# Weight loads of five down products issued by GpSimd instead of SyncE

## The chip, the cores and the metric

The kernel runs on one core of a Trainium2 chip. Its time is the device time of one execution in microseconds, as the median of several runs. A profiled execution gives, beside its time, the span from its first to its last instruction and a trace of all engines: TensorE (PE in the profile), VectorE (DVE), ScalarE (ACT), GpSimd (POOL) and SyncE (SP), and of the 16 DMA engines that move data between HBM and the core's memory for all of them.

## The reference, cut to what matters

```python
def _B_ref(x, W_gate, W_up, W_down):          # D = 1024, F = 3584
    gate = jnp.einsum("bsd,df->bsf", x, W_gate)
    up = jnp.einsum("bsd,df->bsf", x, W_up)
    gate = gate * (lambda x, dt: x.astype(dt))(gate > 0, gate.dtype)
    h = gate * up
    return jnp.einsum("bsf,fd->bsd", h, W_down)
...
x = A_x                                        # 1 x 2048 x 1024, bfloat16
x = x + _A_ref(_layernorm(x, axis=-1), A_wqkv, A_wo)
x = x + _B_ref(_layernorm(x, axis=-1), B_W_gate, B_W_up, B_W_down)
x = x + _A_ref(_layernorm(x, axis=-1), A_wqkv, A_wo)
x = x + _B_ref(_layernorm(x, axis=-1), B_W_gate, B_W_up, B_W_down)
return x
```

Layer A is a linear attention with 32 heads, layer B a gated MLP. The kernel counts its four layers from 0, so the last layer, a B, is layer 3.

## The kernel before, in words

The residual x (2048 rows) stays in the core's memory, with rows sent away to HBM and brought back where the room is needed. A B layer goes over the rows in two chunks c of 1024. For each chunk, `glu` runs over 14 blocks u of 256 columns of F, two hidden parts per block, and computes h transposed; then `down` multiplies h by W_down. All large products are cut by Strassen's scheme (seven products of quarters in place of eight): a weight block is therefore loaded as its raw quarters and as sums of quarters, and the sums that were made in an earlier layer are read back from HBM (`tgu` for the gate and up weights, called tg and tu in the trace; `td` and `dd` for W_down).

A chunk's down phase consists of seven outer products, which for layer 3 stand in the order "11", "T2", "T1", "T3", "22", "21", "T4" (`order_d`). A plain one reads its weights in two loads of 896 KB (`product`, line 1434). A deep one is cut by the scheme once more (`deep`, line 1468): it reads its weights in four loads, three of 896 KB and one of 448 KB (`load_deep`, line 1047), and each load serves two of its seven groups of matmuls, the last one serves one. For layer 3, chunk 0, the products T1, 22, T4 and 21 are deep and 11, T2 and T3 are plain.

The weights of all layers come through one ring (`_Ring`, line 24): a list of loads in the order of use, of which at most five may be in the core at a time. Before a product uses entry i of the list, `free_before` issues the loads up to i + 4; each new load takes a slot that an earlier entry has given up, and the instruction that issues it waits on its engine until TensorE has read that entry. When "21" uses its last entry, T4's last load is issued; when T4 uses its entries, the gate and up weights of the next chunk's first block are issued (`load_gu`, line 1197: the raw part at line 1198, the sums at line 1202).

All these loads are issued by SP, in the order in which the program writes them. In the same queue of SP stand, in this stretch, the transposes of the normalized rows for the second chunk (`ln_turn`, line 423), which wait for ScalarE, and a few reads for inner products (line 1138). The transposed rows are summed on the DVE (`sums_x`, line 1272) for the next chunk's first gate product, `vg`. GpSimd multiplies one quarter of h in each block of `glu` (line 1381) and, in the last layer's down phases, issues most of the output stores (`onto`, line 1464), each of which waits for a DVE addition (line 1463). Work that is not bound to a place in the matmuls is put into a list of delayed jobs (`_Later`) that `later.tick()` runs. The tile framework allots the slots and the semaphores and sets each engine's order of instructions.

Of the kernel before, what the change touches and what calls it, by code (L numbers as in the profile page):

```python
# [12 lines left out]
F16 = mybir.dt.float16  # L13
# [79 lines left out]
class _Net:  # L93
# [889 lines left out]
    def plan_B(self, l):  # L983
        for c in range(2):
            for u in range(self.U):
                for w in "gu":
                    self.ring.add((l, c, w, u), lambda t, w=w, u=u, first=(l == 1 and c == 0),
                                  d=self.is_inner(l, c, u): self.load_gu(t, w, u, first, d))
            for p in self.order_d(l, c):
                if self.is_deep(l, c, p):  # L990
                    for e in range(4):
                        self.ring.add((l, c, p, e), lambda t, p=p, e=e: self.load_deep(t, p, e))
                    continue
                for h in range(2):
                    src = self.src_d(p, slice(h * self.U // 2, (h + 1) * self.U // 2))
                    self.ring.add((l, c, p, h), lambda t, src=src: self.nc.sync.dma_start(
                        out=t[:, 0:self.U // 2, :].bitcast(src.dtype), in_=src))

    T_AT = {"T1": 0, "T3": 1, "T4": 2, "T2": 3}
# [44 lines left out]
        return t[:, :, :].rearrange("p a b -> p (a b)")[:, 0:n].rearrange(  # L1044
            "p (m k n) -> p m k n", m=2, n=NW // 2)

    def load_deep(self, t, p, e):
        n = min(2, 7 - 2 * e)
        self.nc.sync.dma_start(out=self.deep_view(t)[:, 0:n, :, :].bitcast(F16),
                               in_=self.dd[p][:, 2 * e:2 * e + n, :, :])  # L1050

    def load_dd(self, p):
# [755 lines left out]
```

## Time and profile before

| what | value |
|---|---|
| median of 3 runs | 1442.72 us |
| lowest and highest of them | 1442.53, 1443.81 us |
| the profiled execution's own time | 1441.07 us |
| its span | 1439.3 us |
| granted clock | 1.000 |
| DMA traffic over the span | 339.14 MB, 236 GB/s on average |

The span is 1.77 us shorter than the profiled execution's time, and that time is 1.65 us below the median of the runs. In the rows that follow, a timeline's first number is the start in microseconds from the span's start, the second the duration, and a bracket at the end tells how long the engine had been idle and what ended that. "SPq" marks an instruction that SP's queue issues. A row "A <- B: x, n, y" says that A waited for B for x us in all, n times, y at the longest. A DMA's time "to landing" runs from its issue to the moment when all its bytes have arrived.

### The profile page before, as it was taken

Reading aid. Unit: us, or ns where it says so; the run is one execution under the profiler, and the core shown is the slowest. Engines: PE = TensorE matmul, PEld = TensorE weight load, DVE = VectorE, ACT = ScalarE, POOL = GpSimd, SP = SyncE. Lnnn points to the kernel's source line nnn. Section 1 sums busy time; section 2 is a strip of 40 time slices with the busy share of each in tenths; the row PEclk is TensorE's granted clock in tenths of the full one; section 3 lists DMA queues with packets and bytes.
Section 4 is the critical chain, followed back from the end, with each engine's and each line's share of the span. In section 5 each row is a group of like instructions: output and inputs, shape, how many; then the busy total and the mean of one; then the engine's idle time right before and its main releaser. Section 6 shows DMA issues by size and latency. Waiting matters only on the chain.

```text
span 1439.3 us, 21517 instructions
## 1 busy us (share of the span) xinstructions
PE 1426.7 (99%) x7763; PEld 744.3 (52%) x7790; DVE 1052.8 (73%) x2035; ACT 626.0 (43%) x1145; POOL 309.6 (22%) x220
## 2 busy tenths in 40 slices
PE   9999999999999999999999999999999998999998
PEld 4444444444455444545654444445554584555557
DVE  7978698788685666559778885765766874766895
ACT  7872564333334234332058626633442443444301
POOL 1453860010100010110031577410111021111102
PEclk9999999999999999999999999999999999999999
DMA  9950787998559999866983118988878699985575
GB/s 287 239 162 8 174 208 204 291 320 289 195 195 310 353 348 331 273 219 214 293 274 95 60 28 255 284 271 256 263 238 298 204 299 335 314 230 173 191 261 183
DMA packets 366620, 339.14 MB, mean 236 GB/s; under 512 B 110065, under 2 KB 326001, under 8 KB 365489
## 3 DMA queue, kind: packets, MB, share of 16 engines
q1 hardware_dynamic: 357936, 314.95, 73.1%
q10 hardware_dynamic: 7136, 18.88, 3.5%
q0 software_dynamic: 1440, 3.93, 0.8%
q8 instruction: 61, 1.00, 0.3%
q14 instruction: 47, 0.38, 0.1%
HBM read 248.25 MB, written 64.82 MB: 218 GB/s over the span
## 4 chain that ended last, share of the span: by engine, by line
PE 93%; DVE 4%; ACT 1%; issue 1%; DMA 1%; SPq 0%; DVEq 0%; ACTq 0%
PE ps L506 11%; PE yu L1301 9%; PE yg L1301 9%; PE dy L1443 8%; PE xu L1301 6%; PE xg L1301 6%; PE i L1154 5%; PE dx L1443 4%; PE ps L789 4%; PE zu L1301 3%; PE zg L1301 3%; PE my L588 3%; PE dy L1485 2%; PE mv L588 2%; PE mx L588 2%; PE dyT L1485 2%
## 5 line engine op out<-in xcount | busy, mean ns | idle before, releaser
L1301 PEld LDWEIGHTS <-w 128*128 128x128 f16 (+1 forms) x2768 | 270.3, 98 | 299.6 <-issue 4.0
L506 PE MATMUL ps<-w,xnT 128*128 128x512 bf16 x768 | 169.8, 379 | 0.2 <-DVE pq L452 0.2
L1381 POOL TENSOR_TENSOR h<-m5u,m5g 128x512 f16<-128x512 f32 x28 | 37.1, 1326 | 426.8 <-DVE m5u L1377 265.5
L506 PEld LDWEIGHTS <-xnT 128*128 128x128 bf16 x768 | 74.4, 98 | 89.8 <-issue 1.8
L1301 PE MATMUL xg<-xnT,w 128*128 128x512 f16 x448 | 115.4, 379 | 0.2 <-DVE yg L1341 0.2
L1301 PE MATMUL xu<-xnT,w 128*128 128x512 f16 x448 | 115.0, 379 | 0.0
L1485 PEld LDWEIGHTS <-h 128*128 128x128 f16 x1064 | 104.1, 98 | 13.3 <-issue 0.2
L1381 POOL TENSOR_TENSOR h<-c22u,c22g 128x512 f16<-128x512 f32 x28 | 35.6, 1271 | 290.2 <-DVE c22u L1377 237.5
L1301 PE MATMUL yu<-s,w 128*128 128x512 f16 x376 | 96.5, 379 | 0.5 <-DVE zu L1357 0.5
L1301 PE MATMUL yg<-s,w 128*128 128x512 f16 x376 | 96.6, 379 | 0.0
L449 ACT ACTIVATE e<-e,eps 128x512 f32<-128x512 f32 x128 | 91.0, 720 | 3.2
L736 POOL TENSOR_TENSOR kvc<-pq,kvc 128x1024 f32<-128x1024 bf16 x32 | 78.5, 2454 | 53.1 <-DVE den L741 32.8
L1443 PEld LDWEIGHTS <-h 128*128 128x128 f16 x560 | 54.8, 98 | 64.9
L789 PE MATMUL ps<-T,pqT 128*128 128x512 bf16 x374 | 83.0, 379 | 0.5
L1328 DVE TENSOR_TENSOR h<-yu,r 128x512 f16<-128x512 f32 x56 | 38.7, 691 | 54.5 <-PE yu L1301 54.5
L1325 ACT ACTIVATE r<-yg 128x512 f32<-128x512 f32 x56 | 33.4, 597 | 100.3 <-PE yg L1301 100.3
L527 POOL TENSOR_TENSOR kvc<-kvc,slab 128x512 f32<-128x512 f32 x46 | 57.2, 1249 | 76.0 <-DVE slab L452 72.7
L448 ACT ACTIVATE e<-ps 128x512 f32<-128x512 f32 x92 | 54.3, 590 | 29.1 <-PE ps L506 28.5
L1154 PEld LDWEIGHTS <-x 128*128 128x128 f16 x504 | 49.3, 98 | 33.5 <-issue 1.9
L1325 ACT ACTIVATE r<-zg 128x512 f32<-128x512 f32 x56 | 32.9, 587 | 76.0 <-PE zg L1301 76.0
L748 POOL TENSOR_TENSOR pq<-pq,den 128x1024 bf16<-128x1024 bf16 x32 | 61.2, 1911 | 6.8 <-DVE den L743 6.8
L1443 PE MATMUL dy<-w,h 128*128 128x512 f16 x280 | 61.6, 379 | 0.0
(286 smaller groups left out, 2660.7 us busy)
## 6 DMA issues: line engine op xcount, KB each, us to landing
w<-in_B_W_gate_dram SPq DMA_DIRECT2D x56, 512.0 KB, 6.1
w<-in_B_W_up_dram SPq DMA_DIRECT2D x56, 512.0 KB, 5.8
w<-ddT SPq DMA_DIRECT2D x21, 896.0 KB, 6.5
w<-dd SPq DMA_DIRECT2D x21, 896.0 KB, 5.9
w<-td SPq DMA_DIRECT2D x18, 896.0 KB, 5.5
x<-away SPq DMA_DIRECT2D x30, 512.0 KB, 7.7
away<-x SPq DMA_DIRECT2D x24, 512.0 KB, 6.7
dd<-dd SPq DMA_DIRECT2D x21, 448.0 KB, 5.6
```

Of the source, the lines that this page charges most:

```text
L449: self.last_exp = nc.scalar.activation(out=e, in_=e, func=ACT.Exp, scale=-1.0, bias=self.eps6[:, 0:1])
L506: nc.tensor.matmul(by_row(ps), lhsT=self.xnT[l, l_q][:, kt, j * P:(j + 1) * P], rhs=w[:, kt, :].rearrange("p (b i d) -> p i b d", i=R, d=H ...
L588: nc.tensor.matmul(banks[j], lhsT=A(i)[:, j * P:(j + 1) * P], rhs=B(i), start=start and i == 0, stop=i == NS - 1, skip_group_check=True)
L736: nc.gpsimd.tensor_tensor(out=prod, in0=pq_of[sc, j], in1=zrow, op=ALU.mult)
L748: nc.gpsimd.tensor_tensor(out=heads(pq), in0=heads(pq), in1=den[:, :].unsqueeze(2).to_broadcast([P, D // HD, HD]), op=ALU.mult)
L789: nc.tensor.matmul(ps, lhsT=pqT[sc][:, g, j * P:(j + 1) * P], rhs=T[g // 4][:, g % 4, n2 * NW:(n2 + 1) * NW], start=(g == 0), stop=(g == G ...
L1154: nc.tensor.matmul(b[:, w, :], lhsT=B[p][:, w, k, :], rhs=A[p][:, k, :], start=start and w == 0 and k == 0, stop=k == 1, skip_group_check= ...
L1301: nc.tensor.matmul(ps, lhsT=W[w][m][:, k, :], rhs=A[m][:, k, :], start=start and k == 0, stop=k == 3, skip_group_check=True)
L1325: self.last_relu = nc.scalar.activation(out=out, in_=ps, func=ACT.Relu)
L1381: nc.gpsimd.tensor_tensor(out=h[:, 3, :], in0=V["u"], in1=V["g"], op=ALU.mult)
L1443: nc.tensor.matmul(banks[j], lhsT=A(k)[:, j * P:(j + 1) * P], rhs=w[:, i, :], start=start and k == 0, stop=k == self.U - 1, skip_group_che ...
L1485: nc.tensor.matmul(out, lhsT=A[i // 2][:, i % 2, j * P:(j + 1) * P], rhs=B[m][:, i, :], start=start and i == 0 and j == 0, stop=i == NK - ...
```

## The change

In the last layer's first chunk the loads of five of the seven down products, T1, T3, 22, 21 and T4, are issued by GpSimd's queue instead of SP's: four loads for each of the deep ones and two for T3, 18 in all. The loads of 11 and T2, all loads of other layers and chunks, the gate and up weights and the transposes stay on SP. Bytes, slots, order of use and arithmetic are as before.

```diff
+            queue = lambda p: self.nc.gpsimd if (l, c) == (3, 0) and p not in ("11", "T2") else self.nc.sync
             for p in self.order_d(l, c):
                 if self.is_deep(l, c, p):
                     for e in range(4):
-                        self.ring.add((l, c, p, e), lambda t, p=p, e=e: self.load_deep(t, p, e))
+                        self.ring.add((l, c, p, e), lambda t, p=p, e=e, q=queue(p): self.load_deep(t, p, e, q))
                     continue
                 for h in range(2):
                     src = self.src_d(p, slice(h * self.U // 2, (h + 1) * self.U // 2))
-                    self.ring.add((l, c, p, h), lambda t, src=src: self.nc.sync.dma_start(
+                    self.ring.add((l, c, p, h), lambda t, src=src, q=queue(p): q.dma_start(
                         out=t[:, 0:self.U // 2, :].bitcast(src.dtype), in_=src))
...
-    def load_deep(self, t, p, e):
+    def load_deep(self, t, p, e, queue):
         n = min(2, 7 - 2 * e)
-        self.nc.sync.dma_start(out=self.deep_view(t)[:, 0:n, :, :].bitcast(F16),
+        queue.dma_start(out=self.deep_view(t)[:, 0:n, :, :].bitcast(F16),
                                in_=self.dd[p][:, 2 * e:2 * e + n, :, :])
```

## The prediction

> **What bounds the kernel now.** I read the cores and the busy shares first, then who TensorE waited for over the whole span, and then the stretch of the change in the timelines of PE, SP and POOL.
>
> ```profile
> core 0: 1439.3 us, clock 1.000
> ```
>
> ```profile
> PE 1426.7 (99%) x7763; PEld 744.3 (52%) x7790; DVE 1052.8 (73%) x2035; ACT 626.0 (43%) x1145; POOL 309.6 (22%) x220
> ```
>
> TensorE is busy for 1426.7 of 1439.3 us at the full clock, so only its few waits can be won. They are listed by length; the first two carry this case:
>
> ```profile
> PE vg L1301 <- DMA w<-tg: 2.1, 1, 2.1
> PE vu L1301 <- DMA w<-tu: 1.6, 1, 1.6
> ```
>
> Each happens once. The timeline of PE shows where (the third product of "21" starts at 1171.94, the first of "T4" at 1176.52, the one that needs T4's third load at 1182.63, the one that needs its fourth at 1185.69):
>
> ```profile
> 1171.94 1.69 PE L1485 MATMUL dy<-w,h 128*128 128x256 f16 x14
> ...
> 1176.52 1.69 PE L1485 MATMUL dxT<-w,h 128*128 128x256 f16 x14
> ...
> 1182.63 1.69 PE L1485 MATMUL dyT<-w,h 128*128 128x256 f16 x14
> 1184.16 1.69 PE L1485 MATMUL dzT<-w,h 128*128 128x256 f16 x14
> 1185.69 1.69 PE L1485 MATMUL dyT<-w,h 128*128 128x256 f16 x14
> 1189.47 1.04 PE L1301 MATMUL vg<-s,w 128*128 128x512 f16 x4 [2.09 <-DMA w<-tg]
> 1190.35 1.03 PE L1301 MATMUL xg<-xnT,w 128*128 128x512 f16 x4
> 1192.93 1.04 PE L1301 MATMUL vu<-s,w 128*128 128x512 f16 x4 [1.56 <-DMA w<-tu]
> ```
>
> The down phase ends at 1185.69 + 1.69 = 1187.38. Then the last layer's second chunk opens with two waits on its first gate and up sums: 2.09 + 1.56 = 3.65 us. That is all this change can win, 0.25% of the time. In SP's queue over the same stretch:
>
> ```profile
> 1165.71 0.45 SPq L1049 DMA_DIRECT2D w<-ddT  x1
> 1166.25 0.39 SPq L1138 DMA_DIRECT2D x<-tg  x1
> 1168.87 0.32 SPq L1049 DMA_DIRECT2D w<-ddT  x1
> 1169.43 4.32 SPq L423 DMA_TRANSPOSE xnT<-xnb  x1
> 1173.84 1.67 SPq L1049 DMA_DIRECT2D w<-ddT  x2
> 1175.60 3.95 SPq L423 DMA_TRANSPOSE xnT<-xnb  x1
> 1179.64 1.43 SPq L1198 DMA_DIRECT2D w<-in_B_W_gate_dram  x1
> 1181.12 3.85 SPq L1202 DMA_DIRECT2D w<-tg  x1
> 1185.07 0.41 SPq L1198 DMA_DIRECT2D w<-in_B_W_up_dram  x1
> 1185.53 0.61 SPq L1202 DMA_DIRECT2D w<-tu  x1
> ```
>
> The four T4 loads (w<-ddT), the last transposes and the gated weights share one queue in order. The gate's loads leave at 1179.64 and 1181.12, though the slot they take is the one that "21" gives up when T4 starts, at 1176.52; tu leaves only at 1185.53. SP is held mostly inside long issues (3.95, 3.85), so by the queue's backlog rather than by the count of its instructions. The same stretch in windows (last two numbers: DMA share and GB/s):
>
> ```profile
> 1156.00:1168.00 12.00, 12.00 (x111) 10.67 (x110) 11.73 (x33) 8.15 (x17) 3.40 (x5) 1.00 1.07 307
> 1168.00:1180.00 12.00, 11.96 (x110) 10.58 (x109) 6.93 (x15) 5.82 (x11) 2.85 (x4) 1.00 1.07 323
> 1180.00:1193.00 13.00, 9.35 (x77) 7.13 (x76) 6.92 (x14) 1.50 (x3) 2.85 (x4) 1.00 1.12 323
> ```
>
> The 16 DMA engines are full (share over 1, since packets overlap) up to the moment when tu lands. The line of busy tenths for 1180 to 1192, 0.3 us a digit, has one hole, about three digits long, just as the last transpose drains:
>
> ```profile
> DMA  9969959999999000599999999999889999899898
> ```
>
> So the bytes ahead of tu, not only their order, set when it lands.
>
> **The change part by part.** Five products move: T1, 22, 21 and T4 with four loads each and T3 with two, 18 issues, from SP to POOL. Bytes, slots, and the instructions of PE, DVE and ACT stay. Products "11" and "T2" stay on SP.
>
> *Off SP.* 18 issues of 0.3 to 0.7 us go. What matters is the end: without the two w<-ddT rows at 1173.84 the last transpose can leave about 1.7 us earlier, the gate's load at the slot's release, about 1176.6 instead of 1179.64, and up and tu once T4's first load has been used by two groups, at 1176.52 + 2 x 1.53 = 1179.6, so about 1180.4 instead of 1185.53. If tu then took as long to land as now (1192.93 - 1185.53 = 7.4) it would be there at 1187.8, in time, and the 3.65 us would be gone. That is the gain's end. The other end is nothing: the DMA engines are full, so everything due before vu still has to pass first and tu lands at 1192.9 as now. I am nearest to the second, by the windows: a reordering inside a full resource doesn't shorten the sum. The DVE sums that vg also needs are no obstacle:
>
> ```profile
> 1186.11 0.43 DVE L1272 TENSOR_TENSOR s<-xnT 128x512 f16<-128x512 f16 x1 [1.05 <-DMA xnT<-xnb]
> ```
>
> They end at 1186.54, before 1187.38, and come earlier if the transposes do.
>
> *Onto POOL.* POOL does no arithmetic in this phase; it issues 16 output stores, each of which waits for the DVE. As issue costs I take a store's:
>
> ```profile
> L1464 POOL DMA_DIRECT2D out_dram<-xo x16: 540/710/725, 1151.5 to 1189.0; - x16
> ...
> DMA to landing us min/median/max: 3.8/5.8/7.8
> ```
>
> 18 x 0.71 = 12.8 us of POOL, beside everything, if POOL has nothing else to do; if it had, its stores would go out that much later, and nobody waits for their landing but the program's end, 250 us on. What the move does cost is position: a load now stands behind the stores written before it. Two cases are short:
>
> ```profile
> 1162.74 0.71 POOL L1464 DMA_DIRECT2D out_dram<-xo  x1 [6.13 <-DVE xo L1463]
> ...
> 1173.57 0.71 POOL L1464 DMA_DIRECT2D out_dram<-xo  x1 [5.90 <-DVE xo L1463]
> ```
>
> The third load of "21" stands behind the store at 1162.74, so it leaves at 1163.45 and is wanted at 1171.94: 8.5 us. T4's third load leaves behind the store at 1173.57, at 1174.3, and is wanted at 1182.63: 8.3 us. The loads between stand behind stores too, or only behind a slot, and have as much or more. T1, T3 and the first of "22" are issued in a stretch without stores and lie beside the long products T2 and T3.
>
> How long does such a load take from POOL? No row shows 896 KB on that queue. Over the 16 deep loads on SP, and over T4's four alone:
>
> ```profile
> DMA to landing us min/median/max: 3.3/7.0/10.0
> ```
>
> ```profile
> L1049 SPq DMA_DIRECT2D w<-ddT x4: 319/386/710, 1165.7 to 1175.2; - x4
> ...
> DMA to landing us min/median/max: 8.6/9.3/10.0
> ```
>
> T4's third load, issued at 1173.84, lands 8.6 later at 1182.4, 0.2 before it is wanted: even now there is no slack left. Bounds for POOL: below, 3.3, the quickest on SP; above, the slowest store, 7.8, plus the 768 KB more than its 128 KB at 307 GB/s, 2.6, together 10.4. I take 9.3, the same size under the same load. Each pass of the ring of five (once for "21", once for T4) is then late by at most 9.3 - 8.4 = 0.9 us, 1.8 in all. TensorE reaches the gate's first product at 1189.2 instead of 1187.38 and finds tg there or nearly so (before: 1189.47); tu comes at 1192.9 as the full DMA engines allow. The two small waits in T4 stand in for the first one at vg. At 10.4 the lateness is 2 x 2.0 = 4.0 against the 3.65 that it replaces: +0.4. At 3.3 nothing is late.
>
> *Weighed against the skill.* The rows: with the DVE busy for 11.73 of 12 us (1156 to 1168) POOL's five issues took 3.40 us, 0.68 each; with it busy for 6.92 of 13 (1180 to 1193) four took 2.85, 0.71 each. The DVE does not hold them up. From the rows alone nothing is added. The Trainium skill, SBUF — State Buffer, in its box on the DVE-blocks-DMA trap, says that a DMA issued from GpSimd cannot have its descriptors written while the DVE runs a two-port fast-mode instruction; its example grows from about 0.62 to about 3.1 us. By that figure (an estimate from that page) each load would come some 2.5 us later and the sum would be about +3 us; the rows above don't show it for small stores.
>
> **The sum**, against the profiled execution: span 1439.3, and 1441.07 with what lies around it; the median of the three runs, 1442.72, is 1.65 above that execution. Off SP: 0 (to -3.65). Onto POOL: up to 1.8 us of new waits inside T4 and "21", in place of the old ones at the gate. Net 0: 1441.07 as a profiled time, 1442.7 as a median.
>
> **The rivals.**
>
> *The whole stall goes.* The queues serve each other's gaps, T4's loads stay in time and tu is there at 1187.8: 1442.72 - 3.65 = 1439.1. For it: SP's issues of 3.95 and 3.85 us, the hole in the DMA line, POOL stores that land in a median of 5.8 beside SP loads that take 9.3. Against it: DMA share at 1.07 to 1.12. The Trainium skill, DMA: Bandwidth & Descriptors, under queues, rings and completion order, has each DMA engine take turns between the queues by packet; by that rule T4's loads would pass the transposes in SP's queue, which would help this rival.
>
> *The load is slow from POOL, slower than before.* One mechanism: issue to landing of an 896 KB load on POOL's queue, in the stretch from 1156 to 1186. Lateness is twice what exceeds 8.4 us, less the 3.65 that it replaces; it reaches +2.9 us at 8.4 + (3.65 + 2.9) / 2 = 11.7 us. At 12.5 it gives 2 x 4.1 - 3.65 = +4.6, 1447.3. For it: no slack in T4 now, in-order stores ahead. Against: the bound of 10.4.
>
> *Slow issue on POOL.* The rows price an issue of 128 KB only. If the issue grew with the bytes, 896 KB would take 7 x 0.71 = 5.0 us, 4.3 more, and the load would land after 9.3 + 4.3 = 13.6: 2 x 5.2 - 3.65 = +6.8, 1449.5. Against it: 0.68 and 0.71 us at a full and at a half busy DVE, and SP's issues of the same loads at 0.3 to 0.7 us. The Trainium skill's trap, weighed above, would work in this place. It counts with the slower cases.
>
> **How the numbers follow.** 0.2%, about 2.9 us, is what a measurement of this kernel can tell from no change. No change within it: 0.58. The whole stall or nearly all of it gone: 0.17. Slow from POOL: 0.20, and the slow issue 0.05, so 0.25 for slower. The time is that of the likeliest, 1442.7, whose own range is 1440 to 1445. The range over the cases reaches down to 1439.1, where the stall is used up, and up to 1447, which leaves out the worst of the slow landing and the slow issue.
>
> **What would show it.** Right: 18 w loads as POOL issues of about 0.7 us; up and tu leaving SP near 1180; the waits on tg and tu smaller; new waits of TensorE on T4's or 21's loads (w<-ddT, w<-dd) of under 2 us together; the second chunk's first vu at about 1192.9. Wrong: POOL's loads landing in over 11.7 us or in under 8; an issue on POOL of several us; vu before 1190; POOL's loads ahead of the stores that I put before them; a wait elsewhere in the span that was not there.

## The result, and the profile after

The changed kernel is slower. Its median is 1450.27 us (11 runs, 1447.1 to 1455.89) against 1442.53 us for the kernel before (11 runs, 1440.29 to 1443.81): a ratio of 1.006, 95% interval 1.0046 to 1.0073; the medians lie 7.7 us apart. The ratios, here and below, go by all runs and not by the medians, and leave out one run that was far slower than the others of its kernel (3480.02 us, in experiment 2). The profiled execution took 1449.57 us. The lines of kernel.py behind the edit are one higher than before (L1464 is the DVE's addition, L1465 the store, L1486 a deep product's matmul, L1302 the gate's and up's). The cores view of the kernel after:

```profile
core 0: 1447.7 us, clock 0.998
```

The span grew by 1447.7 - 1439.3 = 8.4 us. Who TensorE waited for over the whole span, after the change:

```profile
PE vg L1302 <- DMA w<-tg: 2.7, 1, 2.7
PE dyT L1486 <- DVE xo L1464: 2.3, 1, 2.3
PE dyT L1486 <- DMA w<-ddT: 1.6, 1, 1.6
...
PE vu L1302 <- DMA w<-tu: 1.3, 2, 1.2
```

The two waits at the gate are still there (2.7 and 1.2, before 2.1 and 1.6), and two new ones stand ahead of them, inside T4. The timeline of PE of the kernel after, from T4's third load to the gate, and the last matmul of the span:

```profile
1184.60 1.70 PE L1486 MATMUL dyT<-w,h 128*128 128x256 f16 x14 [1.56 <-DMA w<-ddT]
...
1190.08 1.69 PE L1486 MATMUL dyT<-w,h 128*128 128x256 f16 x14 [2.25 <-DVE xo L1464]
1194.47 1.04 PE L1302 MATMUL vg<-s,w 128*128 128x512 f16 x4 [2.70 <-DMA w<-tg]
1195.34 1.86 PE L1302 MATMUL xg<-xnT,w 128*128 128x512 f16 x4
1198.37 1.89 PE L1302 MATMUL vu<-s,w 128*128 128x512 f16 x4 [1.17 <-DMA w<-tu]
1200.05 1.91 PE L1302 MATMUL xu<-xnT,w 128*128 128x512 f16 x4
1201.76 1.26 PE L1302 MATMUL xg<-xnT,w 128*128 128x512 f16 x4
1202.86 1.03 PE L1302 MATMUL yg<-s,w 128*128 128x512 f16 x4
...
1441.79 0.93 PE L1486 MATMUL dvT<-w,h 128*128 128x256 f16 x7
```

The rows of the kernel before that answer to the last two:

```profile
1195.53 1.03 PE L1301 MATMUL yg<-s,w 128*128 128x512 f16 x4
...
1434.48 0.93 PE L1485 MATMUL dvT<-w,h 128*128 128x256 f16 x7
```

So yg starts 7.33 us later (1202.86 - 1195.53), and so does the last matmul (1441.79 - 1434.48 = 7.31): nothing between them costs anything. The 8.4 us divide like this:

- Waits. 1.56 + 2.25 + 2.70 + 1.17 = 7.68 us in place of 2.09 + 1.56 = 3.65: **+4.0**.
- Clock. Four matmuls of 128x512 take 1.03 us at the full clock; here groups of four take 1.86, 1.89 and 1.91, and the granted clock from 1193 to 1199 is 0.70 (before: 1.00). From vg to vu it was 3.46 us before with a wait of 1.56, so 1.90 of work; now 3.90 with a wait of 1.17, so 2.73: 0.83 more. From vu to yg it was 2.60, now 4.49: 1.89 more. Together **+2.7**.
- The end. From the last matmul's end to the end of the span it was 1439.3 - 1435.41 = 3.9 us, now 1447.7 - 1442.72 = 5.0: **+1.1**.
- The rest, 8.4 - 4.0 - 2.7 - 1.1 = 0.6 us. Of it 0.24 lies ahead of T4's third load (the group ahead of that load's starts at 1181.35, in the kernel before at 1181.11). The other part lies in T4's two waits: each row overlaps the next by 0.16 us while nothing waits, so that the starts move by 1.73 and 2.42 us where the rows give 1.56 and 2.25 as idle.

Where do the waits come from? The issues are as meant. The timeline of POOL of the kernel after has T4's third and fourth load at 1172.44 and 1175.70, each of 0.55 us and not held up by a store:

```profile
1172.44 0.55 POOL L1050 DMA_DIRECT2D w<-ddT  x1 [2.48 <-PE dx L1486]
1173.80 0.72 POOL L1465 DMA_DIRECT2D out_dram<-xo  x1 [0.81 <-DVE xo L1464]
...
1175.70 0.55 POOL L1050 DMA_DIRECT2D w<-ddT  x1
```

TensorE, which waits for the third, goes on at 1184.60: 12.1 us from issue to landing. The transposes in SP's queue are slower still. The timeline of SP of the kernel after (the first row holds the last two of the eight transposes), and below it the landing times of the last six transposes, as the line's own view gives them:

```profile
1169.67 9.63 SPq L423 DMA_TRANSPOSE xnT<-xnb  x2
1179.39 0.53 SPq L1135 DMA_DIRECT2D x<-gi  x1
1180.09 1.96 SPq L1199 DMA_DIRECT2D w<-in_B_W_gate_dram  x1
1182.10 5.63 SPq L1203 DMA_DIRECT2D w<-tg  x1
...
1188.40 2.18 SPq L1203 DMA_DIRECT2D w<-tu  x1
```

```profile
DMA to landing us min/median/max: 5.7/7.8/16.8
```

SP issues tu at 1188.40, not near 1180 as the change meant, and 2.9 us later than before, since it is held in the issue of the last transpose and in tg's. tg leaves at 1182.10, 1.0 us later than before (1181.12), and takes 12.3 us to land (before: 8.3). The DVE is held too. Its additions `xo` take their room from the same buffers as the rows that the transposes read, and wait until a transpose has let one go. Two rows of the DVE's timeline, the second of which ends TensorE's wait of 2.25:

```profile
1186.59 0.69 DVE L1464 TENSOR_TENSOR xo<-x,dxT 128x512 bf16<-128x512 f32 x1 [4.34 <-DMA xnT<-xnb]
1189.34 0.69 DVE L1464 TENSOR_TENSOR xo<-x,dyT 128x512 bf16<-128x512 f32 x1 [2.06 <-DMA xnT<-xnb]
```

So weights and transposes came late together, though no bytes were added. The windows of the kernel after (last three numbers: granted clock, DMA share, GB/s) show the DMA engines as full as before, moving less:

```profile
1168.00:1180.00 12.00, 11.96 (x110) 10.58 (x109) 7.17 (x15) 5.84 (x11) 4.60 (x8) 1.00 1.15 263
1180.00:1193.00 13.00, 7.96 (x70) 6.49 (x68) 5.70 (x12) 0.60 (x1) 2.27 (x4) 1.00 1.09 284
1193.00:1199.00 6.00, 3.36 (x10) 1.09 (x11) 1.12 (x4) 1.18 (x2) 0.57 (x1) 0.70 1.11 360
```

263 and 284 GB/s stand in place of 323 and 323. In slices of 0.6 us from 1168 to 1192 the row of GB/s shows how that comes about, first of the kernel after, then of the kernel before:

```profile
GB/s 356 367 312 440 419 375 413 391 423 491 399 324 219 61 39 47 37 50 29 65 75 126 61 373 360 369 317 361 425 344 195 265 138 87 362 335 363 328 290 324
```

```profile
GB/s 336 295 40 11 136 358 351 473 423 372 554 308 382 466 481 197 293 340 223 428 504 360 369 410 388 312 19 7 200 318 292 335 382 423 319 337 341 304 405 382
```

After the change ten slices in a row, from 1175.8 to 1181.8, lie at 29 to 126 GB/s; I call this the crawl. Before, there are two dips of two slices each. The DMA queues of the kernel after from 1175.4 to 1181.4 (packets, MB, share of 16 engines) tell what the engines were busy with; a packet counts, with its whole duration, where it starts:

```profile
q1 hardware_dynamic: 702, 0.17, 116.0%
q0 software_dynamic: 44, 0.25, 22.9%
```

q1 is SP's queue, q0 POOL's. In these 6 us the transposes' packets of 256 bytes take all the engines' time: 1.16 x 16 x 6.0 us / 702 = 159 ns for each on average. POOL's queue, with the rest of T4's weights in it, moves 0.25 MB in 44 packets, one for every 16 of the transposes'. From 1150 to 1168, beside POOL's loads of "21" and T4's first, the queue of SP, which then held little but transposes, looks like this in the same kernel:

```profile
q1 hardware_dynamic: 5654, 1.40, 48.8%
```

That is 0.488 x 16 x 18.0 / 5654 = 25 ns a packet. Slow packets aren't new, though. SP's queue in the second dip of the kernel before, from 1183.6 to 1184.8:

```profile
q1 hardware_dynamic: 48, 0.02, 143.0%
```

1.43 x 16 x 1.2 / 48 = 572 ns each, but for 48 packets only. So a dip of some 1.2 us belongs to the kernel before as well; new is a stretch of 6 us.

### The profile page after: what moved, and what is told of

The parts are those of the page before. It is cut to its first block, busy times and chain, and to the rows that moved or that the text cites. A ratio compares the mean times of both kernels' runs of the same rounds, so it can differ in the third digit from the quotient of the medians.

```text
span 1447.7 us, 21559 instructions
## 1 busy us (share of the span) xinstructions
PE 1430.5 (99%) x7790; PEld 743.9 (51%) x7790; DVE 1052.1 (73%) x2035; ACT 626.3 (43%) x1145; POOL 319.4 (22%) x238
## 4 chain that ended last, share of the span: by engine, by line
PE 89%; DVE 5%; DMA 2%; issue 2%; ACT 1%; POOL 1%; SPq 0%; DVEq 0%; POOLq 0%; ACTq 0%
PE ps L506 11%; PE yu L1302 9%; PE yg L1302 9%; PE dy L1444 7%; PE xu L1302 6%; PE xg L1302 6%; PE i L1155 5%; PE dx L1444 4%; PE ps L789 4%; PE zg L1302 3%; PE zu L1302 3%; PE my L588 3%; PE mv L588 2%; PE mx L588 2%; PE dyT L1486 2%; PE vu L1302 2%
## 5 line engine op out<-in xcount | busy, mean ns | idle before, releaser
L1302 PEld LDWEIGHTS <-w 128*128 128x128 f16 (+1 forms) x2768 | 270.8, 98 | 302.3 <-issue 6.8
L1302 PE MATMUL xg<-xnT,w 128*128 128x512 f16 x448 | 116.5, 382 | 0.2 <-DVE yg L1342 0.2
L1302 PE MATMUL xu<-xnT,w 128*128 128x512 f16 x448 | 115.9, 381 | 0.0
L1486 PEld LDWEIGHTS <-h 128*128 128x128 f16 x1064 | 104.0, 98 | 17.6 <-issue 2.4
L1302 PE MATMUL yu<-s,w 128*128 128x512 f16 x376 | 96.5, 379 | 0.5 <-DVE zu L1358 0.5
L1302 PE MATMUL yg<-s,w 128*128 128x512 f16 x376 | 96.6, 379 | 0.0
```

The costliest lines, as they stand in the source:

```text
L1302: nc.tensor.matmul(ps, lhsT=W[w][m][:, k, :], rhs=A[m][:, k, :], start=start and k == 0, stop=k == 3, skip_group_check=True)
L1486: nc.tensor.matmul(out, lhsT=A[i // 2][:, i % 2, j * P:(j + 1) * P], rhs=B[m][:, i, :], start=start and i == 0 and j == 0, stop=i == NK - ...
```

## The experiments

The first theory: the transposes in SP's queue and T4's loads in another queue, in flight together, make the crawl (crossing theory). Rivals: the new order of SP's queue, in which a read of 512 KB (x<-gi) now stands ahead of the gate's weights; and GpSimd's queue as such, slow for loads of this size. The kernel before, run beside them, had medians of 1441.82 us (the first four), 1441.67 (the next four) and 1441.87 (the last four).

**1. The change without transposes.** The eight transposes of the second chunk are plain copies of the same bytes in the same pieces of 256 bytes; they leave the transposition out.

```diff
+        if (layer, q // 2) == (3, 1):
+            nc.sync.dma_start(out=self.xnT[layer, q][:, :, j * P:(j + 1) * P],
+                              in_=xn[:, :].rearrange("p (k r) -> p k r", r=P))
+            return
         nc.sync.dma_start_transpose(out=self.xnT[layer, q][:, :, j * P:(j + 1) * P], in_=xn)
```

> The changed kernel, but the eight transposes of the last layer's second chunk are plain copies of the same rows on the same queue (256 KB each, runs of 256 bytes), so that chunk computes with rows that are not turned. Crossing theory (transposes in SP's queue and weight loads in POOL's queue together bring the DMA engines to a crawl): the crawl at 1176 to 1182 is gone, no load of POOL takes over 10 us, TensorE's waits at the end of the down phase are 4 us or less and the time is 1441 to 1445. GpSimd theory (loads from POOL are slow in themselves): T4's loads still take 12 us and the time stays at 1448 to 1452. Order theory (the read of x<-gi that moved ahead of the gate's weights is the loss): that order stays, so 1448 to 1452 too.

1441.54 us, ratio 0.9996 (0.9987 to 1.0006). All 18 loads still leave from POOL, and the crawl is gone. Its windows:

```profile
1168.00:1180.00 12.00, 11.96 (x111) 10.56 (x109) 8.02 (x18) 6.25 (x11) 5.52 (x9) 1.00 1.05 375
1180.00:1193.00 13.00, 10.77 (x89) 8.31 (x87) 6.94 (x15) 1.78 (x3) 2.86 (x4) 1.00 1.06 365
```

GpSimd's queue as such is not slow: without transposes T4's loads land in 6.7 to 8.0 us, and TensorE waits for none of the 18.

**2. The kernel before without transposes.** The same edit in the kernel before.

> The kernel before with the same eight plain copies in place of transposes (the second chunk of the last layer computes with rows that are not turned): the measure for the run above. All theories: 1438 to 1443, that is, no more than the 3.65 us of the two waits can be won. If plain copies are as dear as transposes, no change.

1438.57 us, ratio 0.9979 (0.9969 to 0.9988). So the change beside plain copies still costs 1441.54 - 1438.57 = 3.0 us, 0.2%. The two profiles, 3.6 us apart in their spans, show 1.1 us of it at the end and waits at the gate of 1.8 + 0.4 us against 0.6; the rest, some 0.8 us, lies ahead of this stretch, where one of them has a wait of 1.1 us for weights of the attention. The likely reason of the waits at the gate is the read of x<-gi, which now stands ahead of the gate's weights in SP's queue; no run shows it alone. The other 7.7 - 3.0 = 4.7 us of the change's loss need the transposes.

**3. T4's loads back on SP.** The other four products stay on POOL.

```diff
-p not in ("11", "T2") else self.nc.sync
+p not in ("11", "T2", "T4") else self.nc.sync
```

> The changed kernel with T4's four loads back on SP; T1, T3, 22 and 21 stay on POOL, and x<-gi stands behind the gate's weights as before. Crossing theory: the two last transposes have no POOL loads beside them; at most 2 us slower than before, 1442 to 1445, of which 0.9 is the longer closing drain of POOL (14 issues more at 0.06). GpSimd theory: the loads of 21 are late too, T4's are not: 1444 to 1448. Order theory: as before but for the drain, 1442.5 to 1444.

1444.1 us, ratio 1.0027 (1.0002 to 1.0053; one run of ten took 1460.27 us). The crawl is gone (356 and 325 GB/s in the two windows), and TensorE waits 1.5 us on tg and 2.1 on tu, 3.6 us as in the kernel before. Its rows of SP and of PE are worth a look:

```profile
1181.63 2.78 SPq L1203 DMA_DIRECT2D w<-tu  x1
```

```profile
1193.05 1.04 PE L1302 MATMUL vu<-s,w 128*128 128x512 f16 x4 [2.11 <-DMA w<-tu]
1193.92 1.68 PE L1302 MATMUL xu<-xnT,w 128*128 128x512 f16 x4
1195.39 1.91 PE L1302 MATMUL xg<-xnT,w 128*128 128x512 f16 x4
```

tu leaves 3.9 us earlier than in the kernel before (1185.53), and vu starts no earlier (1193.05, before 1192.93). And the clock falls for some matmuls behind these waits (1.91 us for four; granted 0.72 from 1193 to 1199), which it didn't behind 2.09 + 1.56. x<-gi is back behind the gate's weights here too, so the order theory is not yet out.

**4. The order of SP's queue.** The change, with x<-gi and the reads of its kind held back behind the gated weights.

```diff
+            self.last_gu = self.nc.sync.dma_start(out=t[:, 4:8, :][:, b, :].bitcast(F16), in_=self.tgu[w, u][:, b, :])
...
+                if (l, c) == (3, 1) and u + 2 == us[0]:
+                    at(10, lambda m=m: self.behind(self.last_gu, lambda m: self.load_gi(m, u + 2), (m,)))
+                else:
                     at(10 if u + 2 == us[0] else 1, lambda m=m: self.load_gi(m, u + 2))
```

> The changed kernel with the reads x<-gi, x<-tg and x<-tu for the first inner products held behind the third block's gate weights in SP's queue, as they stood before the change. Order theory: most of the loss is gone, 1443 to 1446. Crossing theory: T4's loads are as late as in the changed kernel and the DVE waits as long; only the 0.6 MB less ahead of tu is won, 1 to 2 us: 1448 to 1450.

1448.87 us, ratio 1.0059 (1.0033 to 1.0084). The crawl stays (256 GB/s from 1168 to 1180, 193 from 1180 to 1193), and TensorE's largest wait is now on T4's load:

```profile
PE dyT L1486 <- DMA w<-ddT: 4.8, 1, 4.8
PE vu L1302 <- DMA w<-tu: 2.0, 1, 2.0
```

The order theory falls: the read ahead of the gate's weights is not what costs most.

**5. T4 alone on POOL.**

```diff
-p not in ("11", "T2") else self.nc.sync
+p == "T4" else self.nc.sync
```

> Only T4's four loads on POOL, the other 14 back on SP. Crossing theory, sharpened (the crawl comes where the last two transposes lie beside T4's loads from POOL): T4's third load takes 12 us or more, 1446 to 1450, and the closing drain of POOL takes 3.65 + 4 x 0.06 = 3.9 us. If a backlog that all five products build up on POOL's queue is needed: no crawl, 1442 to 1444.

1448.96 us, ratio 1.0052 (1.0037 to 1.0067). Four loads of the 18 suffice. The crawl comes earlier (191 GB/s from 1168 to 1180, under 150 GB/s from 1169.8 to 1177.0): it begins while the sixth transpose is in flight (14.8 us to landing), and T4's fourth load leaves only after it, at 1179.99. What stands behind the slow transpose in SP's queue is now the last load of "21" (18.6 us):

```profile
PE dy L1486 <- DMA w<-dd: 8.7, 1, 8.7
```

**6. All 18 loads on ScalarE's queue instead of POOL's.**

```diff
-queue = lambda p: self.nc.gpsimd if
+queue = lambda p: self.nc.scalar if
```

> All 18 loads as in the changed kernel, but issued by ScalarE, whose queue is a hardware queue like SP's. Crossing of any two queues: the crawl is there too, 1446 to 1452, and POOL's drain is back at 3.65. A matter of GpSimd's queue alone: no crawl, 1440 to 1444, as long as ScalarE is not held up by waiting for slots; if it is, TensorE waits for ACT and not for DMA.

1465.18 us, ratio 1.0152 (1.0125 to 1.018): worse. From 1168 to 1180 the engines move 96 GB/s at a share of 1.07:

```profile
1168.00:1180.00 12.00, 7.61 (x69) 6.42 (x66) 3.31 (x8) 2.67 (x5) 0.17 (x1) 1.00 1.07 96
```

So the loads need not stand in GpSimd's queue for a crawl; in ScalarE's they do it too, with the stores still in GpSimd's. TensorE waits 7.3 us for `xo`, an addition that waits for a transpose (6.57 us). ScalarE's own work is held by the issues as well: TensorE waits 3.1 us for its evictions.

**7. T4's third and fourth load on SP, the other 16 on POOL.**

```diff
-e=e, q=queue(p): self.load_deep(t, p, e, q))
+e=e, q=self.nc.sync if p == "T4" and e > 1 else queue(p): self.load_deep(t, p, e, q))
```

> The changed kernel with only T4's third and fourth load back on SP, behind the last two transposes. Sharpened crossing theory: while the last two transposes drain, nothing but stores is on POOL's queue, so no crawl: T4's loads land within 10 us, 1442 to 1445, of which 1.0 is the drain. If T4's first two loads beside the last but one transpose are enough: a shorter crawl, 1445 to 1448.

1445.9 us, ratio 1.0026 (1.0017 to 1.0035). No crawl (348 and 359 GB/s; one dip of three slices, 106, 46 and 38), and TensorE waits 0.6 us on tg and 3.3 on tu; the clock is at 0.72 from 1193 to 1199. This narrows the place: the crawl of the changed kernel hangs on the two loads at 1172.44 and 1175.70.

**8. Only the last two transposes as plain copies.** Otherwise the changed kernel.

```diff
+        if layer == 3 and t in (11, 15):
+            nc.sync.dma_start(out=self.xnT[layer, q][:, :, j * P:(j + 1) * P],
+                              in_=xn[:, :].rearrange("p (k r) -> p k r", r=P))
+            return
```

> The changed kernel with only the last two of the eight transposes (rows of tiles 11 and 15) made plain copies, so those rows are not turned; the first six transposes stay beside the loads of 22 and 21 on POOL. Sharpened crossing theory: no crawl at 1176, 1441 to 1445. If any transpose beside POOL's loads costs: the first six still do, 1445 to 1449.

1441.9 us, ratio 1.0001 (0.9991 to 1.0012). Windows, and SP's queue from 1175.4 to 1181.4:

```profile
1168.00:1180.00 12.00, 11.96 (x111) 10.57 (x109) 7.31 (x16) 6.00 (x11) 4.77 (x8) 1.00 1.06 381
1180.00:1193.00 13.00, 10.97 (x86) 8.04 (x84) 6.92 (x14) 1.97 (x4) 2.85 (x4) 1.00 1.07 364
```

```profile
q1 hardware_dynamic: 1599, 0.40, 30.6%
```

Packets of the same size take 0.306 x 16 x 6.0 / 1599 = 18 ns each, a ninth of the 159 ns of the transposes' packets. The other six transposes still cross the loads of "22" and "21" on POOL, and TensorE waits for none of these loads.

Experiments 7 and 8 take away the one side and the other of the same pair, and each ends the crawl. That six other crossings are harmless here, and that in experiment 5 the sixth transpose is slow beside T4's first loads, says that the pair is not the whole condition. The last four ask what else belongs to it.

**9. The change without the first chunk's output stores.** The additions stay; half of the output isn't written.

```diff
+                if (l, c) != (3, 0):
                     queue.dma_start(out=self.o_v[:, ts.start + s.start:ts.start + s.stop, cols], in_=xo[:, s, :])
```

> The changed kernel, with the output stores of the last layer's first chunk left out (the additions on the DVE stay, half of the output isn't written). If the crawl needs only the crossing of transposes in SP's queue with weight loads in GpSimd's, it is still there: 30 to 110 GB/s somewhere between 1174 and 1182, the last two transposes at 13 to 17 us to landing, TensorE waiting some 6 to 8 us on T4's loads, xo and tg. The time would then be about 1447 to 1449: GpSimd's closing drain falls by 16 DMAs x 0.06 = 1.0 us. If the 128 KB stores in GpSimd's queue belong to what starts it, the last two transposes land in 8 to 10 us, no T4 load takes over 10, and the time is about 1441 to 1443.

1440.8 us, ratio 0.9999 (0.9989 to 1.0008). The pair is still crossed. GB/s in slices of 0.6 us from 1168 to 1192, SP's queue from 1174.0 to 1176.4 and in the two lowest slices, 1174.6 to 1175.8, and the landing of the transposes issued from 1158 on:

```profile
GB/s 382 416 349 377 382 394 311 394 406 294 163 31 34 134 438 383 396 371 210 58 283 111 79 306 252 103 111 294 353 337 306 346 326 371 347 301 329 380 343 344
```

```profile
q1 hardware_dynamic: 709, 0.18, 119.3%
```

```profile
q1 hardware_dynamic: 39, 0.01, 97.4%
```

```profile
DMA to landing us min/median/max: 5.3/6.7/11.3
```

1.193 x 16 x 2.4 / 709 = 65 ns a packet, between the 18 and the 159, and in the lowest slices 0.974 x 16 x 1.2 / 39 = 480 ns. What is left there is a dip of two slices like those of the kernel before (31 and 34 GB/s, there 40 and 11), with single low slices later (58, 79). T4's loads land in 6.9 to 8.8 us, and the gate's waits are 2.9 + 0.6 us. So the first expectation failed, and the second came nearly true: with the stores of 128 KB in POOL's queue the dip becomes a crawl of 6 us. Whether it is their queue or only their bytes and their time, this run can't tell.

**10. The last two transposes on ScalarE's queue, the loads on POOL.**

```diff
-        nc.sync.dma_start_transpose(
+        (nc.scalar if layer == 3 and t in (11, 15) else nc.sync).dma_start_transpose(
```

> The changed kernel, with the last two transposes (rows of tiles 11 and 15) issued by ScalarE's queue instead of SP's; the weight loads stay on GpSimd. If what counts is that transposes and weight loads are in different queues, whichever they are, the crawl stays: 1446 to 1452, with transposes of 13 us or more. If it counts that SP's queue holds transposes and gated weights behind them, the gated weights are now free of them, the waits on tg and tu go, and the time is about 1440 to 1443.

1452.57 us, ratio 1.0077 (1.0063 to 1.009). ScalarE's queue (q10) from 1176 to 1182:

```profile
q10 hardware_dynamic: 502, 0.12, 118.8%
```

1.188 x 16 x 6.0 / 502 = 227 ns a packet: the crawl follows the transposes to their new queue. TensorE no longer waits for tg or tu, but 5.3 us for `xo` and 2.1 for ScalarE.

**11. The mirror: the kernel before, its last two transposes on ScalarE's queue.** The same edit, with all weight loads on SP.

> The kernel before (all weight loads on SP), with only the last two transposes moved, to ScalarE's queue. The mirror image of the change: the same two kinds of transfer cross again, with their queues exchanged. By the crossing theory the DMA engines crawl once more between 1168 and 1193 (under 300 GB/s in one of the two windows), a transpose takes over 12 us to landing, and the time is 1445 to 1455. If what counts is that the weight loads leave SP, nothing crawls; the gated weights pass the transposes and the time is 1438 to 1442.

1445.01 us, ratio 1.0032 (1.0018 to 1.0046). The time lies at the low end of what the crossing theory expected, but not for its reason. From 1168 to 1180 the engines move 306 GB/s, from 1180 to 1193 318. ScalarE's queue from 1175.4 to 1181.4, and TensorE's wait:

```profile
q10 hardware_dynamic: 371, 0.09, 7.7%
```

```profile
PE dyT L1485 <- ACT dyT L1494: 3.6, 1, 3.6
```

0.077 x 16 x 6.0 / 371 = 20 ns a packet: no crawl. The transposes are slow to land here as well (up to 16.0 us), though their packets are quick. In the profile the time goes because ScalarE is held 7.6 us in the issue of the last one. So the crossing theory falls in its plain form: here a crossing with the loads in SP's queue and the transposes in another left the throughput as it was. The profiled execution was, however, the fastest of the eleven (1442.84 us); others took up to 1453.12, and whether those crawl is not shown.

**12. Loads and transposes together on ScalarE's queue.** Experiment 6, and the eight transposes there too.

> All 18 loads on ScalarE's queue, as in the run that did that alone (1465.18), and the eight transposes of the second chunk on ScalarE's queue too: both kinds share one queue again, and only the gated weights stay on SP. By the crossing theory the long crawl from 1164 to 1197 goes: windows of 1156 to 1168 and 1168 to 1180 at over 280 GB/s, and at least 10 us less than 1465; a crawl may be left where the last transpose meets the gated weights, after 1177. If it is ScalarE's being held up by its issues that costs, and not the crossing, the time stays at 1460 or above, since ScalarE now has eight more issues to do.

1450.97 us, ratio 1.0065 (1.0051 to 1.0078), 14.2 us less than experiment 6, though ScalarE issues eight transfers more. Its window:

```profile
1168.00:1180.00 12.00, 5.86 (x50) 4.92 (x48) 3.37 (x9) 4.55 (x9) 0.51 (x1) 0.82 1.07 270
```

270 GB/s stand in place of 96, a little under the 280 that I had set. What remains is ScalarE's own delay: TensorE stands for 6.9 us behind additions of the DVE (`dz`) that wait for late evictions.

**What is shown and what stays open.** Shown: most of the cost, 4.7 of 7.7 us, needs the transposes, and it comes with the crawl. In the changed kernel the crawl needs the last two transposes (8), T4's last two loads in a queue apart from theirs (3 and 7), and the output stores (9); with ScalarE's queue the crawl is there with the loads apart from the transposes (6) and the long one goes when they share it (12). In the crawl a transpose's packet takes 159 ns (the changed kernel) or 227 ns (experiment 10) on average instead of some 20; in the kernel before, only a few packets at a time were slow. Open: why a packet takes so long, why the six earlier crossings are harmless, and why the mirror (11) is, where only the queue of the loads differs from experiment 10. No run looks into a DMA engine. None of the kernels that compute the whole is faster than the kernel before.

## Why the prediction was wrong, point by point

*Where the cost is.* The prediction looked at the right place: all but 1.1 us of the 8.4, the end, and 0.24 us ahead of T4 lie between T4's loads and the second chunk's first products.

*"The bytes ahead of tu, not only their order, set when it lands."* Right, by experiment 3: 3.9 us earlier off SP, 0.1 us later at vu. The gain's end (3.65 us) was rightly put aside. But how many bytes pass in a microsecond wasn't fixed, which is the step that failed below.

*Slow issue on POOL.* Didn't happen: 0.53 to 0.58 us per load, below the 0.71 that I took from the stores. The effect that the Trainium skill describes under SBUF — State Buffer, in its box on the DVE-blocks-DMA trap, wasn't seen: from 1156 to 1168, with the DVE busy for 11.72 of 12 us, the loads were issued in 0.54 to 0.58 us, and those of "21" landed in 5.2 to 6.8.

*Position behind the stores.* Wrong and harmless: the third load of T4 left at 1172.44, ahead of the store at 1173.80, and the third of "21" at 1161.63, ahead of the store at 1162.98.

*The step that failed: "How long does such a load take from POOL?"* I took 9.3 us, with 10.4 as the upper bound; T4's third load took 12.1, while the third of "21" took 5.4. The bound added 768 KB at 307 GB/s, so it rested on a rate that I held fixed because the bytes were. That rate was the thing that changed: 29 to 126 GB/s for 6 us. The DMA share at 1.07 to 1.12 could not tell me, since it counts how long packets take and not what they carry; it was 1.15 from 1168 to 1180, with the crawl's first 4.2 us in it. The rival "slow from POOL" had the right sign and nearly the right landing (12.5), but that was luck, since its mechanism was wrong: POOL's queue is quick without the two transposes (experiment 8: T4's loads land in 5.9 to 7.7 us), and the wait came once, 1.56 us in T4, not twice.

*"In place of the old ones at the gate."* This failed too. The sum let the waits in T4 replace those at the gate, since tg and tu would come no later than before. But SP was busy with the last two transposes until 1179.30, so that the gate's loads left at 1180.09 and 1182.10 instead of from 1176.6 on, and tg took 12.3 us to land. The gate's waits stayed, 2.70 + 1.17 = 3.87 us against 3.65, and T4's came on top of them.

*Rule and rows.* My first rival leaned on a rule of the Trainium skill, DMA: Bandwidth & Descriptors, under queues, rings and completion order: each DMA engine takes turns between the queues by packet, so T4's loads would pass the transposes. The rows: the loads did get turns, but from 1175.4 to 1181.4 POOL's queue had 44 packets beside 702 of SP's, so that on average 16 x 159 ns = 2.5 us of a transpose's packets stood between two of the loads'. At the 20 ns a packet of experiment 11 it would have been 0.3 us. How the turns are dealt out the runs don't show. The Trainium skill, DMA: Bandwidth & Descriptors, under rules for kernel authors, says beside a rule on corrupted data that a transpose next to ordinary DMAs needs nothing. It gives no times there; here 1.6 us of waits on T4's load and 2.3 on `xo` show that it can cost time.

*What the sum left out.* Three terms. The transposes' slowness reaches the DVE through the shared buffers and costs 2.25 us, where I had named only T4's weights. The clock costs 2.7 us behind the waits; before, the same place ran at 1.00. And 18 more DMAs on POOL lengthen the end by 1.1 us, where I had written that nobody waits for POOL's landings but the program's end and then charged nothing for that end. Without the crawl the change comes near the net of 0 that I forecast, but not quite: beside plain copies it still costs 3.0 us (experiments 1 and 2). Experiment 8, with its ratio of 1.0001, is no proof of a net of 0, since the kernel before with the same two plain copies, which may be faster too, was not run.

## What to carry to other kernels

Before moving loads to another queue, look at what kinds of transfers stay behind in the old one: bulk loads in another queue than the transposes beside them can lower the throughput of all 16 engines, even if no byte is added. They needn't, as the mirror shows, so measure it. Read GB/s beside the DMA share, in slices of less than a microsecond; a share of 1.1 at 50 GB/s is a stall that looks like work. And count the waits' consequences, the clock behind them and the buffers that a late transfer holds, which here cost more (2.7 and 2.25 us) than the late load itself (1.56).

## What the runs showed of the hardware

- The closing time grows with the DMAs that POOL has issued in the program. From the last matmul's end to the span's end: 3.9 us with 30 of them (before), 4.0 with 34 (experiment 5), 4.8 with 46 (experiment 7), 5.0 with 48 (after): about 0.06 us for each. Without the first chunk's stores it was 4.0 again, with 32 (experiment 9).
- The clock falls to half after waits that are each short. Waits of 1.5 and 2.1 us with 1.9 us of matmuls between them did it (experiment 3), 2.09 and 1.56 didn't (before), nor did 0.4 and 1.8 or 1.7 (experiments 1 and 8). The Trainium skill, TensorE: Matmul & The Clock Gate, under what's actually happening, has two clocks, full and half, and a free-running window of 3.4 us with no work as the cause of the fall. The two clocks agree with the rows (1.03 and 1.91 us for four matmuls); the longest wait of experiment 3 is 2.11 us, shorter than that window, so what else lowers the clock no run here shows.
- The issue of a transfer on SP's or ScalarE's queue can hold the engine for several microseconds: 5.63 us for tg in the kernel after, 7.6 us for a transpose on ScalarE in experiment 11.
